# Slots in pairs, local heads at set points between them, and the low part of the probabilities read from PSUM: an attention and feed-forward kernel on one core

## The chip, the cores and the metric

The kernel runs on one core of one Trainium2 chip. The metric is the device time of one execution in microseconds (us); of several executions the median is taken.

## The reference

Attention over 8 batches, 8 heads, 576 positions and 64 elements a head, then a feed-forward block on its output; all in float32. The first four heads are local, the other four strided:

```python
scores = (q @ k.T) / sqrt(64)                     # per batch and head, 576 x 576
rel = pos[:, None] - pos[None, :]
mask_local   = (rel >= 0) & (rel < 32)            # heads 0 to 3
mask_strided = (rel >= 0) & (rel % 32 == 0)       # heads 4 to 7
attn = softmax(where(mask, scores, -1e9))
x = (attn @ v), laid out as 4608 tokens x 512
out = relu(x @ w_in) ** 2 @ w_out                 # 512 -> 2048 -> 512
```

## The kernel before

The 4608 tokens are cut into 12 chunks of 384. Everything stays on the chip between attention and feed-forward: while the feed-forward of chunk c runs on TensorE (PE), the other engines prepare the attention output x of chunk c+1. To keep float32 accuracy each operand of a large matmul is split into a high part (rounded to fp32r) and a low part (the rest), and three products are made: high by high, low by high and high by low.

**The feed-forward.** A chunk has 16 slots, one for each 128 of the 2048 inner columns. `up(c, j)` (matmul L430) makes one bank h of 128x384 in PSUM by 12 matmuls, four parts of x (xlh, xll from the local heads, xsh, xsl from the strided ones) with three products each. ScalarE (ACT) then makes relu (L435) and square (L436) in place and casts the high part gh (L437); VectorE (DVE) subtracts for the low part gl (L438). `down(c, j)` (L450) adds into three y banks of 128x512 by 9 matmuls, which read gh and gl. gh and gl have two buffers each, h three banks (ps0 to ps2), so a gh is cast when the `down` two slots earlier has read its buffer. The main loop (L565 to L594) writes, for each slot s, `up(s)` and then `down(s-2)`, and then some steps of the attention of the next chunk, spread by a table (SPREAD).

**The local heads.** From the third chunk on, a head is the generator `pe_head`, in six steps between its `yield`s:

- step 0: the DMA loads of q, k, v
- step 1: high and low parts of k and q: ACT casts (kx L214, qx L216), GpSimd (POOL) subtracts (kx L215, qx L217). kx and qx have one buffer each, so a head's can be written only when the scores of the head before it have been read
- step 2: scores s on PE (L231, four matmuls in two banks), mask and negative maximum on DVE (L235, L223)
- step 3: exponentials on ACT (L240), sums on DVE, scaling by ACT (L245; for the fourth head by POOL, L248)
- step 4: vx by ACT and POOL (L251, L252); six DVE transposes of e into p_t (L256); the high part of the probabilities, px, cast by ACT (L262), and their low part subtracted by DVE (L263), with p_t and the high part, both in SBUF, as its inputs
- step 5: outputs o on PE (L273, four matmuls in two banks); each bank is taken off by one ACT copy (L276) and two DVE additions (L277, L278); then xlh by ACT (L280) and xll by POOL (L281)

All banks of scores and outputs come from two, ps3 and ps4, in turn. The helper `local` writes the steps of the four heads interleaved.

**The strided heads.** `strided` has POOL multiply (L380 for scores, L402 for outputs) and DVE reduce (L381, L403), row by row; the products have two buffers. At its end stand transposes on DVE, the cast xsh on ACT (L413) and the subtraction xsl on POOL (L414). It is the bulk of POOL's work.

**The order.** Each engine executes its instructions in the order in which they stand in its queue. Those orders are fixed when the program is built: a scheduler places the operations as their inputs and buffers come free by its own reckoning of durations, with the order of the code as priority, so it may move a head's matmuls between a slot's. `tc.issue_after(i)` binds what is issued within it to come after instruction i in the queue of i's engine.

Chunk 0's feed-forward, the conversion of the weights (about the first 110 us) and the local heads of the first two chunks follow another path.

Of the kernel before, what the change touches and what calls it, by code (L numbers as in the profile page):

```python
# [17 lines left out]
HL = H // 2  # L18
# [66 lines left out]
def attn_moe(ctx: ExitStack, tc, qk_l, v_l, qk_d, v_d, qk_p, v_p, f_s, q_s, k_s, v_s, w_in, w_out, masks, eye, out):  # L85
# [107 lines left out]
    def pe_head(c, h):  # L193
        u = f"{c}_{h}"

        def bank(nm):
            return psum(3 + next(turn) % 2, f"{nm}{u}")

        def buf(pl, nm, n, tag, **kw):
            return pl.tile([P, n], F32, name=f"{nm}{u}", tag=tag, **kw)  # L200

        qk, vp = buf(lraw, "qk", TC + KC, "qk"), buf(lraw, "v", NW * D, "v")
        e = buf(lpool, "e", 512, "e")
        qr, kr = qk[:, :TC], qk[:, TC:]
# [9 lines left out]
        nc.scalar.copy(kx[:, 0, :nk], kr[:, :nk])  # L214
        nc.gpsimd.tensor_sub(kx[:, 1, :nk], kr[:, :nk], f32(kx[:, 0, :nk]))  # L215
        nc.scalar.copy(qx, qr)  # L216
        nc.gpsimd.tensor_sub(qx[D:], qr[D:], f32(qx[D:]))  # L217
        yield
        nmax = small.tile([P, 2 * NW], F32, name=f"nm{u}", tag="nm")
        ssum = sums[h % 3]  # L220
        rs = small.tile([P, 2 * NW], F32, name=f"rs{u}", tag="rs")[:, :NW]
        cut = lambda w: slice(w * kw, (w + 1) * kw)
        reduce = lambda w, src, m: nc.vector.tensor_tensor_reduce(  # L223
            out=e[:QC, cut(w)], in0=src, in1=m, scale=-SCALE, scalar=3.0e38,
            op0=ALU.add, op1=ALU.min, accum_out=nmax[:QC, w : w + 1],
        )
        for a in range(0, NW, 2):
            s_ps = bank(f"s{a}")
            for w in (a, a + 1):
                k0 = wins[w][0]  # L230
                nc.tensor.matmul(s_ps[:QC, 256 * (w - a) : 256 * (w - a + 1)], qx[:, w * QC : (w + 1) * QC], kx[:, :, k0 : k0 + kw], start=True, stop=True)  # L231
            sv = s_ps[:QC].rearrange("p (w t k) -> p w t k", w=2, t=2)
            m = wins[a][1]
            ev = e[:QC, a * kw : (a + 2) * kw].rearrange("p (w k) -> p w k", w=2)
            nc.vector.tensor_add(ev, sv[:, :, 1, :], mask_sb[:QC, m : m + 2, :])  # L235
            for w in (a, a + 1):
                reduce(w, sv[:, w - a, 0, :], e[:QC, cut(w)])
        yield
        for w in range(NW):
            nc.scalar.activation(e[:QC, cut(w)], e[:QC, cut(w)], AF.Exp, bias=nmax[:QC, w : w + 1], scale=-1.0, accum_out=ssum[:QC, w, :1])  # L240
        nc.vector.tensor_reduce(out=rs[:QC], in_=ssum[:QC, :NW], op=ALU.add, axis=AX.X)
        nc.vector.reciprocal(rs[:QC], rs[:QC])
        if h != HL - 1:
# [7 lines left out]
        nc.scalar.copy(vx[:, :, 0, :], vr)  # L251
        nc.gpsimd.tensor_sub(vx[:, :, 1, :], vr, f32(vx[:, :, 0, :]))  # L252
        pt = p_t[h % 2]
        for r in range(QC // STR):
            for k in (r, r + 1):
                nc.vector.transpose(  # L256
                    out=pt[STR * k : STR * (k + 1), :, STR * r : STR * (r + 1)],
                    in_=e.rearrange("p (w k) -> p w k", k=KW)[STR * r : STR * (r + 1), :, STR * k : STR * (k + 1)],
                )
        src = pt.rearrange("p w q -> p (w q)")  # L260
        px = lpool.tile([P, 2, TC], F32R, name=f"px{u}", tag="px")
        nc.scalar.copy(px[:, 0, :], src)  # L262
        nc.vector.tensor_sub(px[:, 1, :], src, f32(px[:, 0, :]))  # L263
        yield
        x = x_tiles(c)
        par, hp = D * (h % 2), h // 2

        src = e[par : par + D, :TC]
        for a in range(0, NW, 2):
            o_ps = bank(f"o{a}")  # L270
            for w in (a, a + 1):
                sl = slice(w * QC, (w + 1) * QC)
                nc.tensor.matmul(o_ps[:, 2 * QC * (w - a) : 2 * QC * (w - a + 1)], vx[:, w].rearrange("p t d -> p (t d)"), px[:, :, sl], start=True, stop=True)  # L273
            ov = o_ps[:, : 4 * QC].rearrange("p (w t q) -> p w t q", w=2, t=2)
            part = src[:, a * QC : (a + 2) * QC].rearrange("p (w q) -> p w q", w=2)
            nc.scalar.copy(part, ov[D:, :, 0, :])  # L276
            nc.vector.tensor_add(part, ov[:D, :, 1, :], part)  # L277
            nc.vector.tensor_add(part, ov[:D, :, 0, :], part)  # L278
        dst = [x["l", s][par : par + D, hp, :] for s in "hl"]
        last["a"] = nc.scalar.copy(dst[0], src)  # L280
        last["g"] = nc.gpsimd.tensor_sub(dst[1], src, f32(dst[0]))  # L281
        yield
# [137 lines left out]
    def up(c, j):  # L420
        x = xt[c]
        p, o = divmod(j, 2)
        ph = psum(j % 2 if c == 0 else (c * NFT + j) % 3, f"h{c}_{j}")
        n = 0
        for kt in range(4):
            kind, kk = "ls"[kt // 2], kt % 2
            xh, xl = x[kind, "h"][:, kk, :], x[kind, "l"][:, kk, :]
            wsl = slice(kt * 256 + o * P, kt * 256 + (o + 1) * P)
            for w, xx in ((wi[p][0], xh), (wi[p][0], xl), (wi[p][1], xh)):
                nc.tensor.matmul(ph[:, :TC], w[:, wsl], xx, start=n == 0, stop=n == 11)  # L430
# [6 lines left out]
        nc.scalar.copy(gh, g)  # L437
        nc.vector.tensor_sub(gl, g, f32(gh))  # L438
        g_tiles[c, j] = gh, gl

    def down(c, j):
        gh, gl = g_tiles.pop((c, j))
# [4 lines left out]
        for t in range(NTT):  # L447
            sl = slice(t * P, (t + 1) * P)
            for k, (g, w) in enumerate(((gh, wo[p][0]), (gh, wo[p][1]), (gl, wo[p][0]))):
                nc.tensor.matmul(y_ps[c][t], g[:, sl], w[:, wsl], start=j == 0 and k == 0, stop=j == NFT - 1 and k == 2)  # L450
        if j == NFT - 1:
            for t in range(NTT):
                y = ypool.tile([P, DM], F32, name=f"ysb{c}_{t}", tag="ysb")
                (nc.scalar.copy if t == 1 else nc.vector.tensor_copy)(y, y_ps[c][t])
                nc.sync.dma_start(out=out[c * TC + t * P : c * TC + (t + 1) * P, :], in_=y)


    def run(gen):
# [37 lines left out]
        return pe_pair(c, pr, local, *b, bank, place % 3)  # L496

    def local(c):
        if c < NPLAIN:
            heads = [pair_at(c, pr, True, pr, "34") for pr in range(2)]  # L500
            turns = (0, 0, 1, 0, 1, 0, 0, 1, 1, 1)
        else:
            heads = [pe_head(c, h) for h in range(HL)]

            turns = [0] * 3
            for h in range(HL):
                turns += [h] + [h + 1] * (3 if h + 1 < HL else 0) + [h] * 2
        for h in turns:
# [55 lines left out]
    NS = NCHUNK * NFT  # L564
    for s in range(NS + 2):  # L565
        c, j = divmod(s, NFT)
        if s < NS:
            up(c, j)
        if s >= 2:
            down(*divmod(s - 2, NFT))  # L570
        if c == 0:
            for _ in range(WRATE):
                if next(weights, "end") != "end":
                    weights_end = {e: last[e] for e in "agsv"}
        if c + 1 < NCHUNK:
            if j == 0:
                lo, st = local(c + 1), strided(c + 1)
                if c == 0:
                    lo, st = behind(heads_end, lo), behind(heads_end, st)
                if c == 1:  # L580
                    lo, st = behind(weights_end, lo), behind(weights_end, st)
# [3 lines left out]
            while dl < fl * (10 if c + 1 < NPLAIN else 6 * HL) and next(lo, "end") != "end":  # L585
                dl += 1
            while ds < fs * cost:
                k = next(st, "end")
# [82 lines left out]
```

## Time and profile before

| | |
|---|---|
| median of 3 runs | 903.34 us (902.61 to 904.56) |
| the profiled execution's own time | 902.66 us |
| its span in the trace | 900.8 us, so 1.9 us lie around it |
| mean granted TensorE clock | 0.982 |
| ACT busy | 564.4 us in 1458 instructions |
| HBM traffic | 78 GB/s over the span |

Times in the trace count from the start of the span. A row of a timeline has start, duration, engine, line, operation, output <- inputs, tile shapes and a count when neighbours of one kind are joined; in brackets stands the idle time before it and what ended it. The matmuls overlap one another, so the pace of PE is read from one start to the next, not from the durations. A row of a line's own view has the shortest, median and longest duration in nanoseconds.

### The profile page before, as it was taken

How to read it: one execution, taken by the hardware profiler on the slowest of the kernel's cores; microseconds unless marked ns; L12 is line 12 of the kernel's file. 1: busy time of each engine (PE TensorE's matmuls, PEld its weight loads, DVE VectorE, ACT ScalarE, POOL GpSimd, SP SyncE). 2: the span in 40 equal slices, each digit the busy share in tenths (PEclk: the TensorE clock that was granted, in tenths of full speed). 3: DMA queues.
4: the chain of work that ended last, by engine and by line, in shares of the span. 5: the costliest groups of instructions: out<-in, count | busy, mean ns of one | idle time of the engine just before them, and what ended most of it. 6: DMA issues, size and time to landing. Idle time of an engine off the chain costs nothing.

```text
span 900.8 us, 14866 instructions
## 1 busy us (share of the span) xinstructions
PE 886.3 (98%) x4744; PEld 800.0 (89%) x4744; DVE 669.5 (74%) x1840; ACT 564.4 (63%) x1458; POOL 693.4 (77%) x724
## 2 busy tenths in 40 slices
PE   8989999999999999999999999999999999999997
PEld 7778899999999999999989989999999999999996
DVE  6789668878877878878878887887886887885111
ACT  3898967657657657747746755755665765764332
POOL 5788577788788889989879997988899799785000
PEclk8599999999999999999999999999999999999999
DMA  9833441323113114102212311221131111000000
GB/s 352 346 123 126 129 150 35 121 69 104 51 51 112 47 48 139 43 13 98 75 32 69 104 31 54 59 86 60 28 110 47 46 46 68 25 1 2 35 1 35
DMA packets 26798, 71.41 MB, mean 79 GB/s; under 512 B 2976, under 2 KB 8736, under 8 KB 25184
## 3 DMA queue, kind: packets, MB, share of 16 engines
q1 hardware_dynamic: 26432, 70.14, 23.4%
q8 instruction: 37, 0.61, 0.3%
q10 hardware_dynamic: 288, 0.33, 0.1%
q14 instruction: 41, 0.34, 0.1%
HBM read 61.01 MB, written 9.44 MB: 78 GB/s over the span
## 4 chain that ended last, share of the span: by engine, by line
PE 86%; POOL 5%; DVE 5%; ACT 2%; issue 1%; DVEq 0%; POOLq 0%; ACTq 0%
PE h L430 41%; PE y L450 40%; POOL pp L402 2%; PE s L231 2%; PE o L273 2%; POOL pq L380 1%; DVE sc L381 1%; DVE px L263 1%; PE b L308 1%; DVE p_t L256 1%; PE w_ps L525 1%; PE b L335 0%; POOL kx L215 0%; DVE e L312 0%; DVE nm L313 0%
## 5 line engine op out<-in xcount | busy, mean ns | idle before, releaser
L450 PE MATMUL y<-w,gh 128*128 128x512 f32 x1152 | 361.9, 395 | 2.4 <-ACT gh L437 2.4
L450 PEld LDWEIGHTS y<-w,gh 128*128 128x128 f32 x1152 | 212.6, 189 | 35.0 <-ACT gh L437 2.6
L430 PE MATMUL h<-xlh,w 128*128 128x384 f32 x768 | 232.7, 342 | 0.4 <-DVE xsl L351 0.4
L430 PE MATMUL h<-xsh,w 128*128 128x384 f32 x768 | 228.1, 337 | 0.0
L402 POOL TENSOR_TENSOR pp<-vs,sc 128x448 f32<-128x448 f32 (+10 forms) x192 | 193.6, 1034 | 39.9 <-issue 21.7
L450 PE MATMUL y<-w,gl 128*128 128x512 f32 x576 | 223.7, 395 | 0.0
L380 POOL TENSOR_TENSOR pq<-ks,qs 128x512 f32<-128x512 f32 (+2 forms) x192 | 200.1, 1063 | 16.0 <-DVE sc L381 12.4
L381 DVE TENSOR_REDUCE sc<-pq 128x8 f32<-128x512 f32 (+4 forms) x228 | 120.1, 535 | 61.4 <-POOL pq L380 59.7
L435 ACT ACTIVATE h<-h 128x384 f32<-128x384 f32 x192 | 91.0, 475 | 112.6 <-PE h L430 111.5
L438 DVE TENSOR_TENSOR gl<-h,gh 128x384 fp32r<-128x384 f32 x192 | 105.4, 549 | 61.4 <-ACT gh L437 59.9
L430 PEld LDWEIGHTS h<-xlh,w 128*128 128x128 f32 x768 | 142.9, 189 | 8.4 <-DVE xsl L351 0.7
L430 PEld LDWEIGHTS h<-xsh,w 128*128 128x128 f32 x768 | 142.5, 189 | 0.5 <-ACT w L169 0.3
L403 DVE TENSOR_REDUCE qs<-pp 128x64 f32<-128x448 f32 (+11 forms) x192 | 106.8, 563 | 31.7 <-POOL pp L402 29.6
L430 PE MATMUL h<-xll,w 128*128 128x384 f32 x384 | 130.3, 339 | 0.0
L430 PE MATMUL h<-xsl,w 128*128 128x384 f32 x384 | 129.2, 336 | 0.0
L450 PEld LDWEIGHTS y<-w,gl 128*128 128x128 f32 x576 | 108.0, 188 | 20.8
L437 ACT CAST gh<-h 128x384 fp32r<-128x384 f32 x192 | 91.2, 475 | 34.1 <-PE y L450 30.3
L436 ACT ACTIVATE h<-h 128x384 f32<-128x384 f32 x192 | 91.0, 474 | 4.5
L240 ACT ACTIVATE e<-e,nm 96x128 f32<-96x128 f32 x160 | 62.6, 392 | 28.3 <-DVE nm L223 27.0
L430 PEld LDWEIGHTS h<-xll,w 128*128 128x128 f32 x384 | 72.8, 190 | 7.5
L256 DVE STREAM_TRANSPOSE p_t<-e 32x128 f32<-32x128 f32 x240 | 72.2, 301 | 4.8 <-ACT e L245 1.4
L430 PEld LDWEIGHTS h<-xsl,w 128*128 128x128 f32 x384 | 72.7, 189 | 0.2
(82 smaller groups left out, 1113.6 us busy)
## 6 DMA issues: line engine op xcount, KB each, us to landing
qk<-qk_l SPq DMA_DIRECT2D x24, 400.0 KB, 3.1
y<-ysb SPq DMA_DIRECT2D x36, 256.0 KB, 2.3
raw<-w_in SPq DMA_DIRECT2D x7, 1024.0 KB, 11.1
qk<-qk_l SPq DMA_DIRECT2D x16, 416.0 KB, 3.1
vs<-v_s SPq DMA_DIRECT2D x10, 576.0 KB, 3.8
raw<-w_out SPq DMA_DIRECT2D x5, 1024.0 KB, 13.3
v<-v_l SPq DMA_DIRECT2D x40, 128.0 KB, 2.0
ks<-k_s SPq DMA_DIRECT2D x8, 576.0 KB, 3.7
```

Of the source, the lines that this page charges most:

```text
L240: nc.scalar.activation(e[:QC, cut(w)], e[:QC, cut(w)], AF.Exp, bias=nmax[:QC, w : w + 1], scale=-1.0, accum_out=ssum[:QC, w, :1])
L256: nc.vector.transpose(out=pt[STR * k : STR * (k + 1), :, STR * r : STR * (r + 1)], in_=e.rearrange("p (w k) -> p w k", k=KW)[STR * r : STR ...
L380: nc.gpsimd.tensor_mul(pv, kt[:, a : a + m, :], qt[:, i - i0 : i - i0 + 1, :].broadcast_to([P, m, D]))
L381: nc.vector.tensor_reduce(out=sc[:, i - i0, a : a + m], in_=pv, op=ALU.add, axis=AX.X)
L402: nc.gpsimd.tensor_mul(pv, vt[:, a : a + nd, :n], sc[:, il : il + 1, :n].broadcast_to([P, nd, n]))
L403: nc.vector.tensor_reduce(out=ot[:, il, a : a + nd], in_=pv, op=ALU.add, axis=AX.X)
L430: nc.tensor.matmul(ph[:, :TC], w[:, wsl], xx, start=n == 0, stop=n == 11)
L435: nc.scalar.activation(g, g, AF.Relu)
L436: nc.scalar.activation(g, g, AF.Square)
L437: nc.scalar.copy(gh, g)
L438: nc.vector.tensor_sub(gl, g, f32(gh))
L450: nc.tensor.matmul(y_ps[c][t], g[:, sl], w[:, wsl], start=j == 0 and k == 0, stop=j == NFT - 1 and k == 2)
```

## The change

1. From the second chunk on the slots go in pairs: `up(s)`, `up(s+1)`, then `down(s-2)`, `down(s-1)`, with `issue_after` binding PE's order.
2. The heads of the next chunk are no longer interleaved by `local` and placed by the scheduler. A table, `plan`, says for each of the chunk's eight pairs which heads take their next step before the ups, between ups and downs, and after the downs; `take` does so and binds the matmuls of scores and outputs to that point of PE's queue. Before or between, the heads' steps are the ones with matmuls: scores of head 0 in pair 0, of head 1 in pair 1, outputs of 0 in pair 2, of 1 in pair 3, scores of 2 ahead of pair 4, of 3 ahead of pair 5, outputs of 2 ahead of pair 6, of 3 ahead of pair 7. The other digits are the steps without matmuls. The first three steps of a chunk's heads (`"010"`) are taken in slot 14 of the chunk before. The spread of the strided heads is as it was.
3. In step 4 ACT also copies p_t into the PSUM bank (`o0`) that the head's first outputs will be written to, and DVE subtracts the high part from that copy instead of from p_t. It makes 40 more ACT instructions (128x384), one for each head of the ten chunks; no other engine's count changes.

Chunk 0's feed-forward and the heads of chunk 1 stand as before. Lines of the changed kernel are 4 to 5 higher: scores L231, copy to PSUM L264, px L265 and L266, outputs L277, their evacuation L280 to L282, xlh L284, xll L285, up L434, gh L441, gl L442, down L455, strided products L384 and L406.

```diff
+        o_ps = bank("o0")
+        nc.scalar.copy(o_ps[:, :TC], src)
         nc.scalar.copy(px[:, 0, :], src)
-        nc.vector.tensor_sub(px[:, 1, :], src, f32(px[:, 0, :]))
+        nc.vector.tensor_sub(px[:, 1, :], o_ps[:, :TC], f32(px[:, 0, :]))
         yield
...
         for a in range(0, NW, 2):
-            o_ps = bank(f"o{a}")
+            if a:
+                o_ps = bank(f"o{a}")
...
+    heads = {}
+    plan = {
+        0: ("", "0", "01"),
+        1: ("", "1", "012"),
...
+        4: ("2", "", "23"),
+        5: ("3", "", "23"),
...
+    def take(c, which):
+
+        if NPLAIN <= c < NCHUNK:
+            for h in map(int, which):
+                if (c, h) not in heads:
+                    heads[c, h] = pe_head(c, h)
+                with ExitStack() as st:
+                    for i in (last["pe"], *(weights_end.values() if c == NPLAIN else ())):
+                        st.enter_context(tc.issue_after(i.ins))
+                    last.pop("mm", None)
+                    next(heads[c, h])
+                    last["pe"] = last.get("mm", last["pe"])
...
-        if s < NS:
+        if s < NFT:
             up(c, j)
-        if s >= 2:
-            down(*divmod(s - 2, NFT))
+            if s >= 2:
+                last["pe"] = down(*divmod(s - 2, NFT))
+
+        elif s % 2 == 0:
+            before, between, rest = plan[j // 2]
+            for part, slots, two in (up, (s, s + 1), before), (down, (s - 2, s - 1), between):
+                take(c + 1, two)
+                with tc.issue_after(last["pe"].ins):
+                    for i in slots:
+                        if 0 <= i < NS:
+                            last["mm"] = part(*divmod(i, NFT))
+                last["pe"] = last["mm"]
+            take(c + 1, rest)
+        if j == NFT - 2:
+            take(c + 2, "010")
```

What it does to the order of the queues is shown at three places. In the names the first number is the chunk, the second the head (of px, vx, o, s, kx, qx, e, xll) or the slot (of h, gh, gl); the last one only numbers the tile.

First, PE around the outputs of head 3 for chunk 7, which are made beside chunk 6's slot 14. Before:

```order
L450 MATMUL y6_2_5809<-w1_5_1117,gh6_11_6341 128x512 x2
L450 MATMUL y6_2_5809<-w1_5_1117,gl6_11_6342 128x512
L430 MATMUL h6_14_6467<-xlh6_5063,w0_7_1174 128x384
L430 MATMUL h6_14_6467<-xll6_5064,w0_7_1174 128x384
L273 MATMUL o07_3_6418<-px7_3_6372,vx7_3_6363 128x192 x2
L273 MATMUL o27_3_6424<-px7_3_6372,vx7_3_6363 128x192 x2
L430 MATMUL h6_14_6467<-xlh6_5063,w0_7_1174 128x384 x2
```

And now:

```order
L455 MATMUL y6_2_5873<-w1_5_1117,gh6_11_6319 128x512 x2
L455 MATMUL y6_2_5873<-w1_5_1117,gl6_11_6320 128x512
L277 MATMUL o07_3_6467<-px7_3_6466,vx7_3_6457 128x192 x2
L277 MATMUL o27_3_6483<-px7_3_6466,vx7_3_6457 128x192 x2
L434 MATMUL h6_14_6491<-xlh6_5106,w0_7_1174 128x384
L434 MATMUL h6_14_6491<-xll6_5107,w0_7_1174 128x384
```

The outputs have moved two matmuls forward, from within slot 14's up to the point just ahead of it; and the tile o0 of head 3 is now numbered next to its px, since it is taken with it.

Second, POOL around kx and qx of head 3 for chunk 11, the last chunk whose heads are made; pp are strided products. Before:

```order
L252 TENSOR_TENSOR vx11_1_9589<-v11_1_9300,vx11_1_9589 128x4x64
L281 TENSOR_TENSOR xll11_9414<-e11_0_9163,xlh11_9413 64x384
L402 TENSOR_TENSOR pp11_5_6_0_9555<-vs11_5_9174,sc11_5_9178 128x448
L402 TENSOR_TENSOR pp11_5_7_0_9558<-vs11_5_9174,sc11_5_9178 128x512
L215 TENSOR_TENSOR kx11_3_9714<-qk11_3_9668,kx11_3_9714 128x416
L217 TENSOR_TENSOR qx11_3_9713<-qk11_3_9668,qx11_3_9713 64x384
L402 TENSOR_TENSOR pp11_5_8_0_9615<-vs11_5_9174,sc11_5_9178 128x288
L402 TENSOR_TENSOR pp11_5_8_32_9618<-vs11_5_9174,sc11_5_9178 128x288
```

And now:

```order
L406 TENSOR_TENSOR pp11_5_10_32_9745<-vs11_5_9282,sc11_5_9286 128x352
L406 TENSOR_TENSOR pp11_5_11_0_9748<-vs11_5_9282,sc11_5_9286 128x384
L285 TENSOR_TENSOR xll11_9477<-e11_1_9176,xlh11_9476 64x384
L406 TENSOR_TENSOR pp11_5_11_32_9751<-vs11_5_9282,sc11_5_9286 128x384
L215 TENSOR_TENSOR kx11_3_9740<-qk11_3_9531,kx11_3_9740 128x416
L217 TENSOR_TENSOR qx11_3_9739<-qk11_3_9531,qx11_3_9739 64x384
L406 TENSOR_TENSOR pp11_5_12_0_9754<-vs11_5_9282,sc11_5_9286 128x416
```

kx and qx of head 3 stood behind the strided product pp 7_0 and now stand behind 11_32, with eight more products, vx of head 2 and xll of head 1 ahead of them.

Third, DVE while the outputs of head 1 for chunk 6 are taken off their banks. Before:

```order
L277 TENSOR_TENSOR e6_1_4951<-o06_1_5251,e6_1_4951 64x192
L381 TENSOR_REDUCE sc7_1_5698<-pq7_1_10_8_5782 128x3
L278 TENSOR_TENSOR e6_1_4951<-o06_1_5251,e6_1_4951 64x192
L256 STREAM_TRANSPOSE p_t0_90<-e6_2_5130 32x4x32 x6
L438 TENSOR_TENSOR gl5_8_5294<-h5_8_5280,gh5_8_5293 128x384
L381 TENSOR_REDUCE sc7_1_5698<-pq7_1_11_0_5785 128x8
L277 TENSOR_TENSOR e6_1_4951<-o26_1_5257,e6_1_4951 64x192
L381 TENSOR_REDUCE sc7_1_5698<-pq7_1_11_8_5830 128x4
L263 TENSOR_TENSOR px6_2_5432<-p_t0_90,px6_2_5432 128x384
L278 TENSOR_TENSOR e6_1_4951<-o26_1_5257,e6_1_4951 64x192
```

And now:

```order
L281 TENSOR_TENSOR e6_1_4806<-o06_1_5151,e6_1_4806 64x192
L385 TENSOR_REDUCE sc7_1_5790<-pq7_1_9_8_5807 128x2
L281 TENSOR_TENSOR e6_1_4806<-o26_1_5230,e6_1_4806 64x192
L282 TENSOR_TENSOR e6_1_4806<-o06_1_5151,e6_1_4806 64x192
L282 TENSOR_TENSOR e6_1_4806<-o26_1_5230,e6_1_4806 64x192
L442 TENSOR_TENSOR gl5_6_5201<-h5_6_5187,gh5_6_5200 128x384
```

The transposes and px of head 2 no longer stand between the four additions; one strided reduce is left among them.

More of the change, by code (lines that the diff above doesn't have):

```diff
@@ L230, in pe_head @@
                 k0 = wins[w][0]
-                nc.tensor.matmul(s_ps[:QC, 256 * (w - a) : 256 * (w - a + 1)], qx[:, w * QC : (w + 1) * QC], kx[:, :, k0 : k0 + kw], start=True, stop=True)
+                last["mm"] = nc.tensor.matmul(s_ps[:QC, 256 * (w - a) : 256 * (w - a + 1)], qx[:, w * QC : (w + 1) * QC], kx[:, :, k0 : k0 + kw], start=True, stop=True)
             sv = s_ps[:QC].rearrange("p (w t k) -> p w t k", w=2, t=2)
@@ L269, in pe_head @@
         for a in range(0, NW, 2):
-            o_ps = bank(f"o{a}")
+            if a:
+                o_ps = bank(f"o{a}")
             for w in (a, a + 1):
                 sl = slice(w * QC, (w + 1) * QC)
-                nc.tensor.matmul(o_ps[:, 2 * QC * (w - a) : 2 * QC * (w - a + 1)], vx[:, w].rearrange("p t d -> p (t d)"), px[:, :, sl], start=True, stop=True)
+                last["mm"] = nc.tensor.matmul(o_ps[:, 2 * QC * (w - a) : 2 * QC * (w - a + 1)], vx[:, w].rearrange("p t d -> p (t d)"), px[:, :, sl], start=True, stop=True)
             ov = o_ps[:, : 4 * QC].rearrange("p (w t q) -> p w t q", w=2, t=2)
@@ L429, in up @@
             for w, xx in ((wi[p][0], xh), (wi[p][0], xl), (wi[p][1], xh)):
-                nc.tensor.matmul(ph[:, :TC], w[:, wsl], xx, start=n == 0, stop=n == 11)
+                done = nc.tensor.matmul(ph[:, :TC], w[:, wsl], xx, start=n == 0, stop=n == 11)
                 n += 1
@@ L439, in up @@
         g_tiles[c, j] = gh, gl
+        return done
     def down(c, j):
@@ L449, in down @@
             for k, (g, w) in enumerate(((gh, wo[p][0]), (gh, wo[p][1]), (gl, wo[p][0]))):
-                nc.tensor.matmul(y_ps[c][t], g[:, sl], w[:, wsl], start=j == 0 and k == 0, stop=j == NFT - 1 and k == 2)
+                done = nc.tensor.matmul(y_ps[c][t], g[:, sl], w[:, wsl], start=j == 0 and k == 0, stop=j == NFT - 1 and k == 2)
         if j == NFT - 1:
@@ L455, in down @@
                 nc.sync.dma_start(out=out[c * TC + t * P : c * TC + (t + 1) * P, :], in_=y)
+        return done
     def run(gen):
@@ L498, in local @@
     def local(c):
[L499 to L508, printed above, removed]
+        heads = [pair_at(c, pr, True, pr, "34") for pr in range(2)]
+        for h in (0, 0, 1, 0, 1, 0, 0, 1, 1, 1):
             next(heads[h])
             yield
+    heads = {}
+    plan = {
+        0: ("", "0", "01"),
+        1: ("", "1", "012"),
+        2: ("", "0", "123"),
+        3: ("", "1", ""),
+        4: ("2", "", "23"),
+        5: ("3", "", "23"),
+        6: ("2", "", "3"),
+        7: ("3", "", ""),
+    }
+    def take(c, which):
[9 more added lines that the diff above has]
+                    last["pe"] = last.get("mm", last["pe"])
     ungated = convert()
@@ L576, in attn_moe @@
             if j == 0:
-                lo, st = local(c + 1), strided(c + 1)
+                lo, st = local(c + 1) if c == 0 else iter(()), strided(c + 1)
                 if c == 0:
@@ L580, in attn_moe @@
                 if c == 1:
-                    lo, st = behind(weights_end, lo), behind(weights_end, st)
+                    st = behind(weights_end, st)
                 cost = sum(2 * sum(range(i0 + 1, i1 + 1)) + 10 for _, i0, i1, _ in ranges(c + 1))
@@ L584, in attn_moe @@
             fl, fs = ((j + 1) / n for n in SPREAD[min(c, 1)])
-            while dl < fl * (10 if c + 1 < NPLAIN else 6 * HL) and next(lo, "end") != "end":
+            while dl < fl * 10 and next(lo, "end") != "end":
                 dl += 1
```

## The prediction

> **What bounds the kernel now.** I read the page first: the busy line, the slices of PE and POOL, the chain that ended last.
>
> ```profile
> PE 886.3 (98%) x4744; PEld 800.0 (89%) x4744; DVE 669.5 (74%) x1840; ACT 564.4 (63%) x1458; POOL 693.4 (77%) x724
> PE   8989999999999999999999999999999999999997
> POOL 5788577788788889989879997988899799785000
> PE 86%; POOL 5%; DVE 5%; ACT 2%; issue 1%; DVEq 0%; POOLq 0%; ACTq 0%
> ```
>
> PE is busy from the fifth slice on to the last; the chain runs through it. POOL is the next: its 77% is 80 to 90% until it runs out of work three slices before the end. A busy PE need not be at its pace, so the second view is PE's timeline within chunk 6:
>
> ```profile
> 402.75 0.33 PE L430 MATMUL h<-xlh,w 128*128 128x384 f32 x1
> 402.92 0.34 PE L430 MATMUL h<-xll,w 128*128 128x384 f32 x1
> ...
> 404.85 0.63 PE L450 MATMUL y<-w,gh 128*128 128x512 f32 x2
> ...
> 406.93 0.64 PE L231 MATMUL s<-kx,qx 128*96 128x256 f32 x4
> 407.41 0.34 PE L430 MATMUL h<-xlh,w 128*128 128x384 f32 x1
> ```
>
> Twelve up matmuls take 404.85 − 402.75 = 2.10 us (0.175 each), nine down matmuls 406.93 − 404.85 = 2.08 (0.231), four of scores 0.48. A slot is 4.18. There is nothing to be had here except where PE falls behind this pace. The waits of PE have one row on the local heads, and the timelines show where it arises:
>
> ```profile
> PE o L273 <- DVE px L263: 1.3, 1, 1.3
> ```
>
> ```profile
> 530.14 2.89 DVE L263 TENSOR_TENSOR px<-p_t,px 128x384 fp32r<-128x384 f32 x1
> ...
> 531.50 0.34 PE L430 MATMUL h<-xll,w 128*128 128x384 f32 x1
> 533.18 0.67 PE L273 MATMUL o<-px,vx 128*128 128x192 f32 x4 [1.34 <-DVE px L263]
> 533.68 0.54 PE L430 MATMUL h<-xlh,w 128*128 128x384 f32 x2
> ```
>
> ```profile
> 459.60 2.59 DVE L263 TENSOR_TENSOR px<-p_t,px 128x384 fp32r<-128x384 f32 x1
> ...
> 461.81 0.51 PE L430 MATMUL h<-xsh,w 128*128 128x384 f32 x2
> 462.33 0.66 PE L273 MATMUL o<-px,vx 128*128 128x192 f32 x4
> ```
>
> ```profile
> 603.57 0.33 PE L430 MATMUL h<-xlh,w 128*128 128x384 f32 x1
> 603.82 0.67 PE L273 MATMUL o<-px,vx 128*128 128x192 f32 x4
> ```
>
> At 531.50 one matmul is followed by the outputs 1.68 us later instead of 0.175: 1.50 lost, since px, begun at 530.14, took 2.89. At 461.81 two matmuls take 0.52 instead of 0.35 (0.17 lost, after a px of 2.59), at 603.57 one takes 0.25 (0.08). The four outputs themselves take 533.68 − 533.18 = 0.50; against
>
> ```profile
> 791.94 0.36 PE L273 MATMUL o<-px,vx 128*128 128x192 f32 x2
> 792.14 0.65 PE L450 MATMUL y<-w,gh 128*128 128x512 f32 x2
> ```
>
> twice 0.20 that is up to 0.10 more at each place. In sum 1.75 to 2.05 us; I take 1.9. Elsewhere in the timeline from chunk 1 on PE keeps its pace; chunk 0's feed-forward, with waits of its own, the change does not touch.
>
> **The change part by part.**
>
> *Pairs.* The switch from down to up is in the row 402.75: the next matmul starts 0.17 later, as between two ups; a switch the other way lies inside the 2.10 and 2.08 above. So fewer switches gain nothing: 0. Nor does ACT lose: a pair's first gh may be cast when the first down is over, 2.08 after the ups, and is read by its own down after the second down and two ups, 2.08 + 4.20 = 6.3 later; cast and subtraction take 0.48 + 0.55 (rows below), so 5.2 us are to spare.
>
> *px from PSUM.* The rows of the lines themselves:
>
> ```profile
> L263 DVE TENSOR_TENSOR px<-p_t,px x40: 540/794/2886, 134.8 to 812.4; 128x384 fp32r<-128x384 f32 x40
> ```
>
> ```profile
> L438 DVE TENSOR_TENSOR gl<-h,gh x192: 509/548/560, 50.9 to 892.0; 128x384 fp32r<-128x384 f32 x192
> ```
>
> ```profile
> L262 ACT CAST px<-p_t x40: 508/514/519, 133.2 to 811.0; 128x384 fp32r<-128x384 f32 x40
> ```
>
> ```profile
> L437 ACT CAST gh<-h x192: 451/479/501, 48.7 to 891.5; 128x384 fp32r<-128x384 f32 x192
> ```
>
> ```profile
> L217 POOL TENSOR_TENSOR qx<-qk,qx x40: 1004/1012/1576, 116.0 to 790.2; 64x384 fp32r<-64x384 f32 x40
> ```
>
> The same subtraction with one input in PSUM (L438) never took over 0.56 in 192 cases beside the same POOL; with both in SBUF it took up to 2.89. The new one is bounded by 0.51 below and 2.89 above; its operands are L438's, so I take 0.55. At 530.14 that saves 2.89 − 0.55 = 2.3, at 459.60 2.0. The added copy on ACT, 40 of them, from SBUF to PSUM, has no row; the nearest are 0.45 to 0.52, so I take 0.5, 20 us in all on an engine busy for 564. It stands ahead of the cast, so px is 0.5 later and then 2.3 shorter where PE had stalled: 1.8 earlier, more than the 1.50 that was lost. Behind the copy in ACT's queue stand the cast, then relu, square and gh of the next slots, with the 5.2 us of room above. So of the 1.9 nothing is left at these places. POOL gains as well: its qx took up to 1.58 against a median of 1.01. I bound what POOL gets back by nothing below and by DVE's own loss above: (0.978 − 0.548) × 40 = 17 us, with the page's mean of 978 ns for L263:
>
> ```profile
> L263 DVE TENSOR_TENSOR px<-p_t,px 128x384 fp32r<-128x384 f32 x40 | 39.1, 978 | 1.0 <-ACT px L262 0.8
> ```
>
> Why the operand decides is told by the Trainium skill, page "SBUF — State Buffer", section "Who interferes with whom": a VectorE operation with two inputs in SBUF and a GpSimd operation that reads SBUF share a port which one of them holds for its whole length, and an operation with at most one input there stays clear of it. The two rows agree (2886 ns against at most 560); by that rule the new subtraction takes L438's time whatever POOL does, while by the rows alone the upper end of 2.89 would stay possible and the stall of 1.50 with it.
>
> *Set points.* Heads 0 and 1 have their scores in pairs 0 and 1 and their outputs two pairs later. A pair is 2 × 2.10 + 2 × 2.08 = 8.36 plus one group of scores or outputs, 0.41 to 0.48: 8.8. So scores to outputs leave 17.2 us for exponentials, transposes and px; scores to the next head's scores 8.4 us for kx and qx, on ACT and POOL. Both look ample on paper, but PE is now bound to the order, and what is late stops it, where before a slot's matmuls could be put ahead. The tightest point is from the outputs of head 1 to the scores of head 2: two downs, 4.16 us, in which both banks must be read. Before, such a reading ran like this (outputs of head 1 of chunk 6):
>
> ```profile
> 440.30 0.32 ACT L276 COPY e<-o 64x192 f32<-64x192 f32 x1 [0.15 <-PE o L273]
> ```
>
> ```profile
> 440.20 1.88 DVE L256 STREAM_TRANSPOSE p_t<-e 32x128 f32<-32x128 f32 x6
> ...
> 445.07 0.35 DVE L278 TENSOR_TENSOR e<-o,e 64x192 f32<-64x192 f32 x1
> ```
>
> From the second bank's copy to the end of the last addition 5.12 us: 0.96 more than 4.16. The ends are thus 0 and 0.96 a place, 0 and 9.6 in ten chunks. The new order has the additions next to one another: 4 × 0.35, one strided reduce and the copies come to some 2.5 us, so I take 0.
>
> Sum: 902.66 − 1.9 = 900.8 for the profiled execution; the median stands 0.7 above it, 903.34 − 1.9 = **901.4**.
>
> **The rivals.**
>
> *No change: small waits at the set points eat the gain.* It needs 1.9 us in ten chunks, so two of ten readings of head 1's banks as slow as before (2 × 0.96), or 0.05 at every one of the 40 set points of scores. For it: the DVE additions stand behind strided reduces that wait for POOL. Against it: the new order above. It gives 903.3. The Trainium skill speaks for this one: in "PSUM — Partial Sum Buffer", section "PSUM bank collisions raise a hardware error ⚠️", two engines must be kept apart within a bank's quarter of the partitions, reads and writes alike, so the bank is closed to scores from the ACT copy until the last addition; no run here shows a collision.
>
> *Slower: kx and qx of head 3 come too late behind the strided products.* The rows of before's POOL and the start of chunk 10 on PE:
>
> ```profile
> 788.98 1.10 POOL L215 TENSOR_TENSOR kx<-qk,kx 128x416 fp32r<-128x416 f32 x1
> 790.16 1.01 POOL L217 TENSOR_TENSOR qx<-qk,qx 64x384 fp32r<-64x384 f32 x1
> ...
> 801.39 5.18 POOL L402 TENSOR_TENSOR pp<-vs,sc 128x384 f32<-128x384 f32 x5
> ```
>
> ```profile
> 753.79 0.33 PE L430 MATMUL h<-xlh,w 128*128 128x384 f32 x1
> ```
>
> In before qx is done at 791.17. The new order puts both behind the product 11_32, the first of the five at 801.39 (1.04 each, so done at 802.43). With kx and qx behind it instead of ahead of it, qx is done at the same 802.4. PE wants those scores after five pairs: 753.79 + 5 × 8.8 = 797.8 by before's clock, 795.9 once the 1.9 is saved. If POOL keeps its pace, PE stands still 6.5 us there, 4.6 net: 903.34 + 4.6 = 907.9. It decides from the point where POOL is less than 6.5 us ahead of its old times. For it: POOL is the fullest engine after PE, and heads 1 and 3 of other chunks may be placed the same way. Against it: POOL gets back up to 17 us from px, and these waits, in the stretch from 126 to 825 us, were tied to PE's and ACT's progress with the heads and may shrink:
>
> ```profile
> POOL xll L281 <- ACT xlh L280: 11.3, 7, 4.0
> ...
> POOL vx L252 <- ACT vx L251: 5.5, 8, 1.4
> POOL kx L215 <- ACT kx L214: 3.6, 4, 2.0
> ```
>
> I take it that POOL comes out ahead by enough rather more often than not.
>
> *A smaller loss of the same kind at the last chunk.* Its strided part was just in time:
>
> ```profile
> 823.48 1.85 POOL L414 TENSOR_TENSOR xsl<-ks,xsh 128x768 fp32r<-128x768 f32 x1 [1.88 <-ACT xsh L413]
> ```
>
> ```profile
> 824.43 0.33 PE L430 MATMUL h<-xlh,w 128*128 128x384 f32 x1
> ...
> 826.88 0.33 PE L430 MATMUL h<-xsh,w 128*128 128x384 f32 x1
> ```
>
> xsl was done at 825.33; before, PE filled up with downs between the parts and came to xsh at 826.88. In the bound order xsl is the eighth matmul: 824.43 − 1.9 + 7 × 0.175 = 823.8. At POOL's old pace that is a wait of 1.6, so 901.4 + 1.6 = 903.0, inside the case of no change.
>
> **How the numbers follow.** A measurement of this kernel can tell about 0.2% from no change, 1.8 us. Forecast, PE at its pace throughout: 0.45. Small waits or the last chunk eat the gain: 0.29. POOL too late: 0.26. The forecast's 901.4 lies just beyond the bound of 901.5, so with a saving between 1.75 and 2.05 two thirds of its chance are faster, 0.31; the part of the middle case in which next to nothing of the 1.9 is lost again adds 0.05: faster 0.36. Of the slower case 0.24 lies beyond 905.1, and 0.02 of the middle one: slower 0.26. The rest, 0.38, is within. The range runs from 900.6 (the 2.05 and some 0.7 for stalls too small to have been seen one by one) to 907.9, the price of POOL's case at its old pace; what is left out is POOL's case repeated in other chunks.
>
> **What would show it.** Right: the changed kernel's px subtraction at a median near 0.55 and a maximum under 0.6; no wait of PE for px; ACT's copy at 0.5; the three places above at PE's pace; and PE's busy time unchanged at 886. Wrong: a row of PE's waits on scores (L231) behind POOL qx or kx, or behind the additions L282, with a microsecond or more; a subtraction that still takes over 1 us; or a strided xsl (L418) that ends after chunk 11's first ups. If the time is under 900, PE's pace itself has changed with the pairs, which the rows above say it does not.

## The result and the profile after

The changed kernel takes 896.89 us (four executions, 896.30 to 897.05) against 903.9 for the kernel before, now of four executions too (902.61 to 904.56): a ratio of 0.992, with a 95% interval of 0.991 to 0.994, so 7.0 us faster. Forecast were 901.4 and a range down to 900.6. The direction was right and the size was not: 2 us foreseen, 7 measured.

The changed kernel's page, busy line and chain:

```profile
PE 878.0 (98%) x4744; PEld 796.8 (89%) x4744; DVE 651.2 (73%) x1840; ACT 577.5 (65%) x1498; POOL 680.2 (76%) x724
PE 90%; ACT 4%; DVE 3%; POOL 1%; DMA 1%; issue 0%; DVEq 0%; POOLq 0%; ACTq 0%
```

PE runs the same 4744 matmuls in 8.3 us less busy time. That is the surprise: a wait that goes away shortens the span, not the matmuls' own time. Of the 8.3 us, 1.7 lie in the start phase (up to the last matmul of tile `b`), and 6.7 behind it, where the granted clock is 1.00 in both kernels, so the clock is not the reason. In each row stand the stretch, its length, the busy time of PE, PEld, DVE, ACT and POOL, the clock, the DMA share and GB/s, first of the kernel before, then of the changed one:

```profile
103.26:901.00 797.74, 791.08 (x4103) 717.75 (x4099) 589.58 (x1677) 484.13 (x1310) 617.48 (x635) 1.00 0.19 61
104.85:896.00 791.15, 784.41 (x4103) 716.11 (x4099) 571.58 (x1677) 497.28 (x1350) 604.25 (x635) 1.00 0.20 61
```

The changed kernel's timeline of PE, a pair in the same region of chunk 6's preparation, shows where it is (only the first row of each slot; in columns, start and duration):

```profile
395.32 0.63 PE L455 MATMUL y<-w,gh 128*128 128x512 f32 x2
...
397.40 0.62 PE L455 MATMUL y<-w,gh 128*128 128x512 f32 x2
...
399.44 0.33 PE L434 MATMUL h<-xlh,w 128*128 128x384 f32 x1
...
401.55 0.33 PE L434 MATMUL h<-xlh,w 128*128 128x384 f32 x1
...
403.63 0.64 PE L231 MATMUL s<-kx,qx 128*96 128x256 f32 x4
```

The pair's first nine down matmuls take 2.08 us, its second nine 2.04; the first twelve up matmuls 2.11, the second twelve 2.08. The first slot after a change of kind is 0.03 to 0.04 us slower than a slot that follows one of its own kind. In the kernel before, every slot was a first one. It is spread over the first six to nine matmuls, at most 12 ns each, with no idle time that a view of waits could show.

To count it over the run, I took each stretch of neighbouring up matmuls, or of down matmuls, from 130 to 820 us of a trace, and summed what its start-to-start times are over the steady ones deep in a long stretch (173.3 ns for an up matmul, 226.7 for a down; a time over 300 ns counts as 300, so that a long wait adds little). The last column is from the last matmul of the start phase (`b`, which the change does not touch) to the last matmul of all.

| kernel | median us | stretches | over the steady pace, us | last b to the end, us |
|---|---|---|---|---|
| before | 903.9 | 427 | 11.98 | 792.0 |
| changed | 896.89 | 158 | 5.56 | 785.2 |
| e1_px_only | 901.57 | 402 | 11.17 | 790.0 |
| e2_no_px | 900.23 | 157 | 6.09 | 789.0 |
| e3_single_slots | 902.55 | 313 | 10.84 | 791.5 |
| e4_pairs_free_heads | 900.36 | 227 | 7.75 | 789.2 |
| e5_threes | 894.35 | 118 | 4.15 | 781.4 |
| e6_bank_turn | 895.01 | 158 | 5.57 | 783.7 |
| e7_threes_bank | 894.45 | 118 | 4.14 | 781.3 |
| e8_threes_shared_g | 895.76 | 119 | 4.19 | 783.3 |

In the three kernels with groups of three, six down matmuls that follow the last `b` elsewhere stand ahead of it. Against the other rows their last column is some 1.5 us too small.

So the two profiled executions, 902.66 and 896.93, differ by 5.7 us:

- stretches −7.1: 11.98 − 5.56 up to 820 us, 1.18 − 0.53 after it
- the waits for px −1.4: 1.75 by the prediction's count (1.50 + 0.17 + 0.08), of which 0.3 is already in the stretches, where a wait counts up to 300 ns
- one new wait +1.4
- the heads' own matmuls from the start phase on +0.3
- the start phase +1.6 (its last matmul at 104.85 against 103.26), which among the seven traces with that order lies anywhere from 103.26 to 104.85
- what follows the last matmul −0.45 (5.08 against 5.53 from its start to the end)

The new wait lies between the two ups of chunk 1's second pair:

```profile
128.40 0.34 PE L434 MATMUL h<-xsh,w 128*128 128x384 f32 x1
129.94 0.45 PE L434 MATMUL h<-xlh,w 128*128 128x384 f32 x1 [1.20 <-DVE gl L442]
```

What was foreseen of px came about, and POOL is ahead of its old times. The changed kernel's own rows for the subtraction and for POOL's qx:

```profile
L266 DVE TENSOR_TENSOR px<-o,px x40: 508/542/558, 135.0 to 807.4; 128x384 fp32r<-128x384 f32 x40
```

```profile
L217 POOL TENSOR_TENSOR qx<-qk,qx x40: 1003/1012/1025, 117.4 to 788.6; 64x384 fp32r<-64x384 f32 x40
```

The longest of 40 subtractions fell from 2886 to 558 ns, the longest qx from 1576 to 1025. The place of the slower rival, kx and qx of head 3 for chunk 11 on POOL and their scores on PE:

```profile
787.47 1.09 POOL L215 TENSOR_TENSOR kx<-qk,kx 128x416 fp32r<-128x416 f32 x1
788.63 1.00 POOL L217 TENSOR_TENSOR qx<-qk,qx 64x384 fp32r<-64x384 f32 x1
```

```profile
793.49 0.63 PE L231 MATMUL s<-kx,qx 128*96 128x256 f32 x4
```

qx is done at 789.6, not at the 802.4 of a POOL at its old pace, and has 3.9 us to spare. PE wants the last strided part at 821.00, and it too was early:

```profile
812.32 1.84 POOL L418 TENSOR_TENSOR xsl<-ks,xsh 128x768 fp32r<-128x768 f32 x1 [2.64 <-ACT xsh L417]
```

It began 11.2 us earlier than before (823.48) and was done 6.8 us ahead of its use; before, it was done at 825.33 and first used at 828.82.

### The profile page after: what moved, and what is told of

It is laid out like the page before. It is cut to its first block, busy times and chain, and to the rows that moved or that the text cites. A ratio compares the mean times of both kernels' runs of the same rounds, so it can differ in the third digit from the quotient of the medians.

```text
span 895.2 us, 14782 instructions
## 1 busy us (share of the span) xinstructions
PE 878.0 (98%) x4744; PEld 796.8 (89%) x4744; DVE 651.2 (73%) x1840; ACT 577.5 (65%) x1498; POOL 680.2 (76%) x724
## 4 chain that ended last, share of the span: by engine, by line
PE 90%; ACT 4%; DVE 3%; POOL 1%; DMA 1%; issue 0%; DVEq 0%; POOLq 0%; ACTq 0%
PE y L455 42%; PE h L434 42%; PE s L231 2%; PE o L277 2%; ACT raw L150 1%; ACT w L169 1%; ACT z L162 1%; PE w_ps L550 1%; DVE z L165 1%; DMA raw<-w_out 1%; DVE e L316 0%; POOL w L170 0%; DVE nm L317 0%; DVE raw L166 0%; DMA vs<-v_s 0%
## 5 line engine op out<-in xcount | busy, mean ns | idle before, releaser
L455 PE MATMUL y<-w,gh 128*128 128x512 f32 x1152 | 355.9, 393 | 5.0 <-ACT gh L441 5.0
L455 PEld LDWEIGHTS y<-w,gh 128*128 128x128 f32 x1152 | 212.8, 189 | 45.8 <-ACT gh L441 5.2
L434 PE MATMUL h<-xlh,w 128*128 128x384 f32 x768 | 230.1, 340 | 1.6 <-DVE gl L442 1.2
L434 PE MATMUL h<-xsh,w 128*128 128x384 f32 x768 | 226.2, 335 | 0.0
L455 PE MATMUL y<-w,gl 128*128 128x512 f32 x576 | 222.2, 392 | 0.0
L406 POOL TENSOR_TENSOR pp<-vs,sc 128x448 f32<-128x448 f32 (+10 forms) x192 | 189.9, 1014 | 39.7 <-DVE qs L407 17.9
L384 POOL TENSOR_TENSOR pq<-ks,qs 128x512 f32<-128x512 f32 (+2 forms) x192 | 198.0, 1050 | 19.1 <-DVE sc L385 15.5
L442 DVE TENSOR_TENSOR gl<-h,gh 128x384 fp32r<-128x384 f32 x192 | 105.5, 550 | 86.9 <-ACT gh L441 85.8
L441 ACT CAST gh<-h 128x384 fp32r<-128x384 f32 x192 | 91.5, 477 | 103.7 <-PE y L455 102.5
L434 PEld LDWEIGHTS h<-xlh,w 128*128 128x128 f32 x768 | 142.7, 189 | 4.8 <-DVE gl L442 1.5
L434 PEld LDWEIGHTS h<-xsh,w 128*128 128x128 f32 x768 | 141.8, 188 | 0.1
L434 PE MATMUL h<-xll,w 128*128 128x384 f32 x384 | 129.7, 338 | 0.0
L434 PE MATMUL h<-xsl,w 128*128 128x384 f32 x384 | 128.6, 335 | 0.1
L455 PEld LDWEIGHTS y<-w,gl 128*128 128x128 f32 x576 | 107.9, 188 | 22.2
L434 PEld LDWEIGHTS h<-xll,w 128*128 128x128 f32 x384 | 72.8, 190 | 2.5
L434 PEld LDWEIGHTS h<-xsl,w 128*128 128x128 f32 x384 | 72.2, 188 | 0.4 <-DVE xsl L355 0.4
## 6 DMA issues: line engine op xcount, KB each, us to landing
raw<-w_in SPq DMA_DIRECT2D x7, 1024.0 KB, 11.2
```

The lines of the kernel that those rows point to most:

```text
L384: nc.gpsimd.tensor_mul(pv, kt[:, a : a + m, :], qt[:, i - i0 : i - i0 + 1, :].broadcast_to([P, m, D]))
L406: nc.gpsimd.tensor_mul(pv, vt[:, a : a + nd, :n], sc[:, il : il + 1, :n].broadcast_to([P, nd, n]))
L434: done = nc.tensor.matmul(ph[:, :TC], w[:, wsl], xx, start=n == 0, stop=n == 11)
L455: done = nc.tensor.matmul(y_ps[c][t], g[:, sl], w[:, wsl], start=j == 0 and k == 0, stop=j == NFT - 1 and k == 2)
```

## The experiments

The theory after the result: a change between up and down matmuls costs PE by itself, and the pairs halve the number of changes. Rivals: px and its contention with POOL made PE slower all along; or the order bound to set points did it.

### Two parts alone

**e1_px_only**: the kernel before with px's low part read from PSUM.

```diff
+        o_ps = bank("o0")
+        nc.scalar.copy(o_ps[:, :TC], src)
         nc.scalar.copy(px[:, 0, :], src)
-        nc.vector.tensor_sub(px[:, 1, :], src, f32(px[:, 0, :]))
+        nc.vector.tensor_sub(px[:, 1, :], o_ps[:, :TC], f32(px[:, 0, :]))
...
```

> Only the low part of the probabilities is read from PSUM; slots and heads are placed as in the kernel before. Theory (the gain comes from fewer changes between up and down matmuls on PE: in the traces from 130 to 820 us, 441 stretches of one kind cost 11.98 us over the steady pace in the kernel before, 158 cost 5.56 in the changed one, so 0.0226 us for each stretch saved): PE's queue here has 490 stretches against 515 before and 217 in the changed kernel, so 0.6 us from them, and the 1.9 us of waits for px: about 901.4. Rival (the contention of px with POOL was the cause of PE's slower pace as well): near the changed kernel, 897 to 898.

Measured 901.57 against 903.87, ratio 0.9975 (0.9965 to 0.9985). All waits of PE for px are gone, as the subtraction shows in this kernel too:

```profile
L265 DVE TENSOR_TENSOR px<-o,px x40: 514/544/558, 139.2 to 813.3; 128x384 fp32r<-128x384 f32 x40
```

This is the theory's price; px alone brings 2.3 us and leaves PE's pace nearly where it was (11.17 over the steady pace against 11.98, and 0.3 of the difference is the waits for px). This is what the forecast had priced, without the pairs. (The 441 stretches named in the expectation are 427 by a right sum, so 0.024 us a stretch.) POOL is busy for 681.7 us instead of 693.4, but its last strided part comes no earlier than the 823.48 of before:

```profile
823.75 1.84 POOL L417 TENSOR_TENSOR xsl<-ks,xsh 128x768 fp32r<-128x768 f32 x1 [1.28 <-ACT xsh L416]
```

**e2_no_px**: the changed kernel with the subtraction from p_t again.

```diff
-        o_ps = bank("o0")
-        nc.scalar.copy(o_ps[:, :TC], src)
         nc.scalar.copy(px[:, 0, :], src)
-        nc.vector.tensor_sub(px[:, 1, :], o_ps[:, :TC], f32(px[:, 0, :]))
+        nc.vector.tensor_sub(px[:, 1, :], src, f32(px[:, 0, :]))
...
```

> Pairs and set points as changed, but the low part read from p_t in SBUF as before. Theory: 217 stretches as in the changed kernel; the heads' outputs have 2.7 us and more to spare at their set points, about as much as the longest px loses, so 0 to 1 us over the changed kernel: 897 to 898; px again up to 2 us and more. Rival (px from PSUM carries the gain): 901 or more.

Measured 900.23, ratio 0.9964 (0.9951 to 0.9976): between the two, 3.3 us over the changed kernel. The pace is the changed kernel's, and no output waits for px. But DVE and POOL lose time again, and the bound order lets it through to PE at other places. The subtraction, two waits on PE and POOL's last strided part in this kernel:

```profile
L263 DVE TENSOR_TENSOR px<-p_t,px x40: 511/836/2177, 129.9 to 808.1; 128x384 fp32r<-128x384 f32 x40
```

```profile
716.56 0.45 PE L231 MATMUL s<-kx,qx 128*96 128x256 f32 x2 [0.49 <-DVE e L278]
```

```profile
825.38 0.44 PE L430 MATMUL h<-xsl,w 128*128 128x384 f32 x1 [0.67 <-POOL xsl L414]
```

```profile
823.50 1.83 POOL L414 TENSOR_TENSOR xsl<-ks,xsh 128x768 fp32r<-128x768 f32 x1 [2.12 <-ACT xsh L413]
```

These are the prediction's rivals of small waits: scores that wait until head 1's bank is read (504, 645 and 716 us), and the last chunk's xsl, as late as in the kernel before. With the waits at 700 and 752 us PE loses 3.5 us (0.32, 0.42, 0.50, 0.73, 0.46 and 1.05, from start to start). The set points need the time that px from PSUM gives back. Both accounts of the expectation were off, the theory's by 2 us.

### The pairs and the set points apart

**e3_single_slots**: set points and px as changed, up and down in turn again.

```diff
-            for part, slots, two in (up, (s, s + 1), before), (down, (s - 2, s - 1), between):
+            for part, slots, two in (up, (s,), before), (down, (s - 2,), between), (up, (s + 1,), ""), (down, (s - 1,), ""):
```

> Set points and px as changed, but the slots of a pair go one by one: up, down, up, down. Theory: 391 stretches against 217, so 174 x 0.0226 = 3.9 us over the changed kernel, 900.8. Rival (the order bound to set points, with no head's matmuls inside a slot, carries the gain): 897.

Measured 902.55, ratio 0.9983 (0.9974 to 0.9992): 5.7 us over the changed kernel, the rival is out. The two kernels differ in the pairs alone. Twice the stretches (313 against 158) cost 10.84 instead of 5.56 us, 0.034 each; my 0.0226 came from the kernel before, whose many short stretches end before the slow matmuls do. No head was late. The wait at chunk 1's start is here as well:

```profile
116.31 0.86 PE L455 MATMUL y<-w,gl 128*128 128x512 f32 x3
118.65 0.44 PE L434 MATMUL h<-xlh,w 128*128 128x384 f32 x1 [1.48 <-DVE gl L442]
```

**e4_pairs_free_heads**: pairs and px as changed, the heads written by `local` and placed by the scheduler as before.

```diff
...
-                lo, st = local(c + 1) if c == 0 else iter(()), strided(c + 1)
+                lo, st = local(c + 1), strided(c + 1)
...
-        if NPLAIN <= c < NCHUNK:
+        if False:
             for h in map(int, which):
...
```

> Pairs and px as changed, but the heads are written and placed as in the kernel before, so that the scheduler puts their matmuls where it likes. Theory: 289 stretches against 217, so 1.6 us over the changed kernel, 898.5, if no head comes late. Rival (set points carry the gain): 901 or more.

Measured 900.36, ratio 0.9964 (0.9952 to 0.9977), 3.5 us over the changed kernel: some 2.2 from 69 more stretches (7.75 − 5.56, heads' matmuls inside slots), and two places where a head's last part was late, some 1.7 us each, less the wait at 128.4, which is not here, and less 0.9 in the start phase. The first of them:

```profile
399.25 0.51 PE L434 MATMUL h<-xlh,w 128*128 128x384 f32 x2
401.30 0.45 PE L434 MATMUL h<-xll,w 128*128 128x384 f32 x1 [1.55 <-POOL xll L285]
```

So the set points are worth 3.5 us beside the pairs; without pairs (e3 against e1) they cost 1.0, of which the wait at chunk 1's start is more than all.

### The cost of a change by itself

**m1_switches**: matmuls only. After a warm-up, in short:

```python
for i in range(16): up(); down()                      # a change every slot
for i in range(8): up(); up(); down(); down()         # every 2 slots
for i in range(4): (up x 4, down x 4)                 # every 4
for i in range(16): up(512); down()                   # both 512 wide
for i in range(16): up(); down(TC)                    # both 384 wide
(up x 16, down x 16)                                  # no change but one
```

> Only matmuls, on five banks, with no wait among them and the other engines idle; attention, activation and all stages of the reference are left out, and the output holds what the last banks show. After a warm-up come six stretches with the same 192 up-like and 144 down-like matmuls each: changing every slot (32 stretches of one kind), every 2 slots (16), every 4 (8), every slot with both kinds 512 wide, every slot with both 384 wide, and not at all. Theory (a change between the two kinds by itself costs PE some 60 to 70 ns there and back): every slot 16 x 0.065 = 1.0 us longer than not at all, every 2 slots 0.5, every 4 slots 0.3. If it is the width that changes the pace, the two stretches of one width cost nothing; if the operands, they cost the same 1.0. Rival (the slower pace after a change comes from the other engines or from waits at the stretch's start): the first three and the last take the same time within 0.1 us.

The windows of these six stretches, in this order (start and end, length, then busy time of PE, PEld, DVE and POOL, PE's clock, the DMA share and GB/s):

```profile
93.21:160.17 66.96, 66.96 (x337) 60.67 (x337) 0.00 (x0) 0.00 (x0) 1.00 0.00 0
160.17:226.62 66.45, 66.45 (x337) 60.51 (x336) 0.00 (x0) 0.00 (x0) 1.00 0.00 1
226.62:292.81 66.19, 66.19 (x337) 60.41 (x336) 0.00 (x0) 0.00 (x0) 1.00 0.00 1
292.81:368.97 76.16, 76.16 (x337) 63.08 (x336) 0.00 (x0) 0.00 (x0) 1.00 0.00 0
368.97:427.24 58.27, 58.27 (x338) 58.27 (x337) 0.00 (x0) 0.00 (x0) 1.00 0.00 1
427.24:493.20 65.96, 65.96 (x337) 60.12 (x336) 2.16 (x4) 0.00 (x0) 1.00 0.02 8
```

With nothing else running, at the full clock, a change every slot costs 66.96 − 65.96 = 1.00 us, every second slot 0.49, every fourth 0.23: some 60 ns there and back each time (1.00 / 16, 0.49 / 8, 0.23 / 4). With one width it costs nothing: 76.16 is 336 × 226.7 ns, 58.27 is 336 × 173.4, although stationary and moving tiles still alternate every slot. So it is the change of the moving operand's width, 384 against 512 (and with it of the output's), and neither the tiles nor any wait. After a change the up matmuls run at 171, 175, 177, 184, 176, 181 and then 173 ns, the down ones at 229, 233, 236, 224, 231, 236, 228, 232, 231 and then 227: the medians at these places in the kernel before are the same to 1 or 2 ns.

**m2_two_inputs**: the subtraction and POOL's products alone and together.

```python
nc.vector.tensor_sub(d, a, b)       # 128x384, both inputs in SBUF
nc.vector.tensor_sub(d, po, b)      # one input in PSUM
nc.gpsimd.tensor_mul(m, ka, kb)     # 128x512
```

> The disputed pair by itself; all of the reference is left out, and the output holds the last tiles. Four stretches: 24 subtractions 128x384 on DVE with both inputs in SBUF, POOL idle; 12 products 128x512 on POOL, DVE idle; 24 such subtractions beside 24 products; 40 subtractions with one input in PSUM beside 24 products. Theory (the second SBUF input is what meets POOL): DVE about 0.54, then up to 1 us or more beside POOL, with POOL's 1.1 us products lengthened too, and 0.54 again from PSUM with POOL at its time alone. Rival (px was long because of something else near it, ACT or DMA): 0.54 in all three.

The rows of the three lines:

```profile
L109 DVE TENSOR_TENSOR d<-pa,pb x48: 543/559/1646, 4.2 to 50.3; 128x384 f32<-128x384 f32 x48
```

```profile
L112 DVE TENSOR_TENSOR d<-po,pb x40: 544/544/557, 44.2 to 68.9; 128x384 f32<-128x384 f32 x40
```

```profile
L115 POOL TENSOR_TENSOR m<-ka,kb x60: 1256/1272/1573, 6.5 to 97.7; 128x512 f32<-128x512 f32 x60
```

Two SBUF inputs take 0.544 us alone and 1.61 beside POOL, whose products take 1.57 instead of 1.27; one input in PSUM takes 0.544 beside POOL, whose products keep their 1.27. The theory holds on both engines. It is also what the Trainium skill says on its page "SBUF — State Buffer", section "Who interferes with whom": the two engines share a port that one holds for a whole instruction. The trace agrees in that the two alternate, one of each every 1.53 us. By length a part still overlaps: alone they follow one another every 0.469 and 1.220 us, 1.69 together.

### Further along the same way

**e5_threes**: groups of 3, 3, 3, 3, 2 and 2 slots, with the set points moved to fit.

```diff
-    gpool = pool("gpool", 2)
+    gpool = pool("gpool", 3)
...
+        0: ("001", "", "", 3),
+        3: ("1102", "", "", 3),
+        6: ("0123", "1", "", 3),
+        9: ("223", "332", "", 3),
+        12: ("", "23", "", 2),
+        14: ("3", "", "", 2),
```

> Slots in groups of 3, 3, 3, 3, 2, 2 in a chunk, three buffers of gh and gl, one buffer of px for the room, heads at set points that fit the groups. Theory: 170 stretches against 217 in the changed kernel, at 0.035 each (5.56 us over 158): 1.6 us less, 895.3. Rival (only the first halving pays, since what a change costs grows with the length of the stretch): 897. If one buffer of px or the new set points make a head late: over 897, with a wait in the profile.

Measured 894.35, ratio 0.9898 (0.9881 to 0.9914), 2.5 us under the changed kernel. 40 stretches fewer gave 1.41 us, 0.035 each as expected. The wait at 128.4 is gone too: chunk 1's second up and most of its third now stand ahead of the first, which needs the late bank; a smaller wait took its place:

```profile
118.17 0.71 PE L231 MATMUL s<-kx,qx 128*96 128x256 f32 x4 [0.37 <-POOL qx L217]
```

**e6_bank_turn**: the changed kernel with the h banks one further.

```diff
-        ph = psum(j % 2 if c == 0 else (c * NFT + j) % 3, f"h{c}_{j}")
+        ph = psum(j % 2 if c == 0 else (c * NFT + j + 1) % 3, f"h{c}_{j}")
```

> The changed kernel with the turn of the three h banks moved on by one, so that chunk 1's first up no longer takes the bank of chunk 0's last. Theory: the one wait that the changed kernel has gained in its trace, at 128.4 us, 1.37 us for h <- DVE gl, goes: 895.5. Rival (gl is late because DVE and ACT are behind at that place whatever the bank): 897.

Measured 895.01, ratio 0.9908 (0.9894 to 0.9923). From the last b to the end it takes 1.5 us less than the changed kernel, and the largest wait of up matmuls is now

```profile
PE h L434 <- DVE xsl L355: 0.4, 1, 0.4
```

which the changed kernel has too. The new wait was the turn of the banks: chunk 0 uses two of them, and its last slot's bank was the first that chunk 1 took. By the intervals alone the two kernels aren't quite apart (0.9923 against 0.9912); the traces are.

**e7_threes_bank** joins both edits.

> Groups of three and the bank turn together. Theory: 896.9 - 1.6 - 1.4 = 893.9. Rival: 896 to 897.

Measured 894.45, ratio 0.9903 (0.9888 to 0.9918): not faster than e5_threes. The two gains don't add, since the groups of three had already lost that wait.

**e8_threes_shared_g**: e7_threes_bank with gh and gl in one tile, whose buffers also serve two of the first chunks' pairs.

```diff
-        gh = gpool.tile([P, TC], F32R, name=f"gh{c}_{j}", tag="gh")
-        gl = gpool.tile([P, TC], F32R, name=f"gl{c}_{j}", tag="gl")
+        gt = gpool.tile([P, 2, TC], F32R, name=f"g{c}_{j}", tag="g")
+        gh, gl = gt[:, 0, :], gt[:, 1, :]
```

> Groups of three and the bank turn, gh and gl as halves of one tile with three buffers, which also serves two of the first chunks' pairs of heads in place of px. Theory: the 1.3 to 2 us that the start up to 106 us had lost in the two kernels with groups of three, where px had one buffer for those pairs too, come back in part: 893. Rival (the start varies by itself by so much): 894.4 as with one buffer.

Measured 895.76, ratio 0.9910 (0.9897 to 0.9924), slower than both accounts. The start had not been lost in the kernels with groups of three, as the expectation took it: their last `b` comes later because six downs stand ahead of it, and the next up begins at 106.40 (e5_threes) and 106.28 (e7_threes_bank) against 106.52 in the changed kernel. Here it begins at 105.74, but now an up waits 0.76 us for gl at 109.55, and the scores of chunk 2's first head wait longer:

```profile
119.48 0.71 PE L231 MATMUL s<-kx,qx 128*96 128x256 f32 x4 [1.28 <-POOL qx L217]
```

The best, e5_threes, is 1.0% under the kernel before.

## Why the prediction was wrong, by its steps

- **Pairs: "So fewer switches gain nothing: 0."** This step failed, and with it the size. It looked at the first matmul after a change, which is indeed no slower (0.17), and took the slot's own 2.10 and 2.08 us for the steady pace. But these slots were all first ones, and nearly all of the cost sits on the second to the ninth matmul. Steady they would be 12 × 173.3 = 2.08 and 9 × 226.7 = 2.04; the 0.02 to 0.04 a slot were inside the figure against which PE was called at its pace. A change of kind was priced at 0; it costs 60 to 70 ns there and back. Fewer changes are worth 6.4 us up to 820 us, 5.3 of them between e3 and the changed kernel, which differ in the pairs alone.
- **px from PSUM.** Right: 0.542 in the median where 0.55 was taken, a maximum of 0.558, the copy within the 0.45 to 0.52 of its nearest rows, and the three waits gone. Alone it brings 2.3 us (e1) where 1.9 stood. The 0.10 more that each group of outputs might have lost did not come back: the heads' own matmuls take 0.3 us more in all, in e1 as in the changed kernel.
- **POOL gets time back.** Right in size: with px alone (e1) POOL is busy for 11.7 us less, between the bounds of 0 and 17. The slower case did not come: qx of head 3 was 12.8 us ahead of the rival's 802.4, and xsl 11.2 us ahead of its old time. But that px decided this is not shown. With px alone xsl begins at 823.75, as late as before, and that qx is done at 791.4 (791.2 before); xsl begins at 823.50 in e2, 822.13 in e3 and 820.42 in e4. Only all three parts together bring 812.32.
- **The bank of outputs of head 1.** Right to take 0 for the kernel as changed; e2 shows that it is no more than just enough, since with px from SBUF the wait appears at three of ten places.
- **Chunk 1's start.** Missed: a new wait of 1.4 us, which e6 traces to the turn of the banks.
- **"If the time is under 900, PE's pace itself has changed with the pairs."** This sentence named the case, and gave it no chance because of the first step.

What stays open is what in PE makes the few matmuls after a change of width slower. m1 shows that the width alone decides, and nothing here shows how. No run has the pairs alone, without set points and without px from PSUM, so what they are worth by themselves in this kernel is not measured.

## What to carry to other kernels

A pace that is read from a stretch in which the pattern never varies holds the pattern's own cost; take the steady pace from a long stretch of one form, or measure it, before an engine is called at its limit. On PE, group matmuls of one moving width: here each pass through another width cost some 60 to 70 ns, which is nothing once and over 6 us a hundred times. And an order that is bound by hand needs its supporting engines to be ahead: with the subtraction from SBUF (e2) PE waited at six places that it passes without a wait in the changed kernel.

## What the runs showed of the hardware that was not expected

- At the full clock a matmul of 128x384 fp32r runs at 173.3 ns from start to start and one of 128x512 at 226.7; after a change from one width to the other the next five to nine are up to 11 ns slower, some 60 ns in sum there and back, with the rest of the core idle (m1_switches).
- Alternating the stationary and the moving tiles without a change of width costs nothing (58.27 us for 336 matmuls of 384, 76.16 for 336 of 512).
- Subtraction and product with two SBUF inputs each, side by side, alternate at 1.53 us a pair, though 0.54 and 1.27 us alone would fit beside each other; both are shown longer, 1.61 and 1.57 (m2_two_inputs). With one input of the subtraction in PSUM they keep 0.544 and 1.27.
